# Token-major attention sums by DMA transposition instead of TensorE products, part of their normalisation on GpSimd, and plain full products instead of column tiles

## The chip, the cores and the metric

The kernel runs on one core of one Trainium2 chip. The metric is the device time of one execution in microseconds (us). Each time is the median of several executions. A ratio is the mean time of one kernel's fast runs over the mean time of the other's fast runs of the same rounds, so it is not quite the ratio of the medians quoted beside it; a 95% interval follows it in brackets. "Faster" and "slower" are verdicts at 2%.

## The reference, cut to what matters

A transformer block of 2048 tokens, width 640, 32 heads of 20, in four segments of 512 tokens. Each segment has causal softmax attention within itself, mixed by a gate with a read-out of a running linear memory of the earlier segments. A projection, two residuals and an MLP of width 1728 follow.

```python
for s in range(4):
    p = softmax(qs @ ks.T * scale + mask)
    a_dot = p @ vs                                  # the "P.V" sums
    num = phi(qs) @ M;  den = phi(qs) @ z + 1e-06   # memory read-out
    o = g * (num / den) + (1.0 - g) * a_dot
    M = M + phi(ks).T @ vs;  z = z + phi(ks).sum()
h  = x + o @ wo
h2 = h + silu(layernorm(h) @ w1) @ w2
```

Inputs and weights are bf16. The softmax denominator is summed as one more column of V and divided out at the end.

## The kernel before

A list of some 400 named tasks fixes the order of all engines; each engine runs its own tasks strictly in that order. A letter in the list picks the engine (`/D` VectorE, `/A` ScalarE, `/G` GpSimd). Heads go in eight groups of four for each segment, so groups 8 to 31 belong to segments 1 to 3. In this document a "group" is one of these.

For a group, TensorE computes P.V in four column tiles, feature-major (features on partitions). ScalarE or VectorE evicts the sums (copies them out of PSUM, the memory of TensorE's results) to `oTs` in SBUF, the working memory, scaled by the gate. TensorE then turns them token-major with identity products, into one PSUM bank, while the memory read-out goes to a second bank. VectorE normalises both halves together, and GpSimd adds them:

```python
def e_tn(eng):                                   # "tn": PE
    for i in range(b0, b1):
        for q, (c, m) in enumerate(bl):          # memory read-out, bank 1
            fns.append(lambda e, ...: e.matmul(bank(pp, 1)[:, V4*i:V4*i+V4],
                lhsT=phiQ[:, c, 128*i:128*i+128], rhs=Mzb[:, m, :], ...))
    for i in range(b0, b1):                      # transposition, bank 0
        fns.append(lambda e, i=i: e.matmul(bank(pp)[:, V4*i:V4*i+V4],
            lhsT=oTs[:, ots.slot, 128*i:128*i+128], rhs=sel, ...))
...
def e_nm(eng):                                   # "nm": DVE, both halves
    T.add(DV, lambda e: e.tensor_tensor(out=r2, in0=v[:, :, :, DH], in1=epsg, op=ALU.add))
    T.add(DV, lambda e: e.reciprocal(out=r2, in_=r2))
    T.add(DV, lambda e: e.tensor_tensor(out=on, in0=v[..., 0:DH], in1=r2, op=ALU.mult))
def e_ad(eng):                                   # "ad": GpSimd
    T.add(PO, lambda e: e.tensor_tensor(out=o_dst, in0=on[0], in1=on[1], op=ALU.add))
```

GpSimd also applies the causal mask ("mk") to the exponentials `PTA`, `PTB`, `PTE`, and P.V waits for that mask.

A full 128x128 product is issued as four column tiles where the neighbouring TensorE tasks are tiled too:

```python
for i, t in enumerate(real):
    before = real[i - 1].mode if i else "r"
    behind = real[i + 1].mode if i + 1 < len(real) else "F"
    t.cm = t.mode == "c" or t.mode == "F" and (before + behind in ("cc", "cr", "rc"))
```

The softmax here doesn't subtract the row's maximum and nothing guards it: scores larger than these inputs give would overflow.

## Time and profile before

| | before |
|---|---|
| time, median of 3 runs | 305.85 us (305.24 to 308.31) |
| TensorE busy, of a span of 306.1 us (the profiled execution took 307.81) | 291.2 us; so it stands still for 14.9 us |
| VectorE, ScalarE, GpSimd busy | 226.1, 220.0, 143.5 us |
| granted TensorE clock | 1.00, but 0.91 from 20 to 60 us |

The prediction below shows the page, the stretches and the timelines. One view that it doesn't show is the waits of TensorE alone. Its columns are: the instruction that waited and what released it, then the us waited in total, the times, and the longest. The first two lines are:

```profile
PE ps_all L896 <- ACT PTE L907: 1.4, 4, 0.7
PE ps_all L530 <- issue: 1.3, 8, 0.2
```

No wait of TensorE in this kernel is worth over 1.5 us, and GpSimd is not among the first ten releasers.

### The profile page before, as it was taken

What the parts mean: (1) busy time and instruction counts of PE and PEld (TensorE: products, weight loads), DVE (VectorE), ACT (ScalarE), POOL (GpSimd) and SP (SyncE); (2) the same over time, 40 slices, a digit from 0 to 9 for tenths busy, and PEclk for the clock granted to TensorE, in tenths of its full rate; (3) what the DMA queues carried; (4) which work ended last, traced back from release to release, by engine and by line L of the source; (5) the groups of instructions that cost most, each with busy time, mean ns of one, the idle gap of its engine ahead of it and who ended that gap; (6) DMA issues with size and microseconds to landing.
All of it is one profiled execution on the core that took longest, in us unless ns stands there. A gap on an engine that the chain in (4) does not pass through costs nothing.

```text
span 306.1 us, 8438 instructions
## 1 busy us (share of the span) xinstructions
PE 291.2 (95%) x3520; PEld 171.2 (56%) x3544; DVE 226.1 (74%) x496; ACT 220.0 (72%) x233; POOL 143.5 (47%) x280
## 2 busy tenths in 40 slices
PE   8989789999999999999999999999999999999996
PEld 6445435546665455576653544546665556764574
DVE  6677767898599896879998978886764696634623
ACT  4689959899989898995899798879768831003500
POOL 6145746375558766281736638464675530300000
PEclk9999879999999999999999999999999999999999
DMA  7949675660455111242433410144052014131002
GB/s 217 329 122 212 141 209 173 120 76 5 76 92 76 22 41 42 39 92 57 88 71 108 78 24 2 21 89 75 5 59 32 2 30 101 46 83 66 0 24 86
DMA packets 48581, 24.72 MB, mean 81 GB/s; under 512 B 38880, under 2 KB 47456, under 8 KB 48544
## 3 DMA queue, kind: packets, MB, share of 16 engines
q1 hardware_dynamic: 48544, 24.19, 35.5%
q8 instruction: 28, 0.46, 0.6%
q14 instruction: 9, 0.07, 0.1%
HBM read 10.41 MB, written 2.62 MB: 43 GB/s over the span
## 4 chain that ended last, share of the span: by engine, by line
PE 66%; DVE 14%; ACT 9%; DMA 6%; issue 3%; SPq 2%; ACTq 0%
PE ps_all L530 44%; PE ps_all L532 8%; PE ps_all L896 6%; PE ps_all L942 4%; DMA beta_bc<-in_A_beta_dram 4%; ACT PTA L907 3%; ACT PTB L907 2%; ACT PTE L907 2%; DMA x_tok<-in_A_x_dram 2%; DVE stt L720 2%; DVE on L1008 2%; PE ps_all L971 2%; DVE phiQ L849 1%; PE ps_all L975 1%; DVE sT L1176 1%
## 5 line engine op out<-in xcount | busy, mean ns | idle before, releaser
L907 ACT ACTIVATE PTA<-ps_all 128x2048 bf16<-128x2048 f32 x32 | 60.1, 1878 | 4.5 <-PE ps_all L896 4.2
L907 ACT ACTIVATE PTB<-ps_all 128x2048 bf16<-128x2048 f32 (+1 forms) x32 | 56.6, 1770 | 8.6 <-PE ps_all L896 8.5
L1170 ACT ACTIVATE th<-ps_all 128x512 f32<-128x512 f32 (+2 forms) x70 | 33.3, 501 | 39.0 <-PE ps_all L530 29.6
L919 POOL TENSOR_SCALAR_AFFINE_SELECT PTB<-PTB 128x512 bf16<-128x512 bf16 x64 | 41.3, 646 | 39.4 <-ACT PTB L907 37.1
L530 PE MATMUL ps_all<-w_sb,sT 128*128 128x320 bf16 x400 | 57.7, 299 | 0.5 <-DVE x_tok L1133 0.5
L530 PE MATMUL ps_all<-hT,w_sb 128*128 128x512 bf16 (+1 forms) x281 | 53.7, 338 | 1.1 <-DVE sT L1176 0.4
L1176 DVE SCALAR_TENSOR_TENSOR sT<-th,ps_all 128x512 bf16<-128x512 f32 (+2 forms) x70 | 37.8, 558 | 21.0 <-ACT th L1170 19.9
L530 PEld LDWEIGHTS ps_all<-w_sb,sT 128*128 128x128 bf16 x400 | 37.9, 98 | 17.6 <-issue 1.7
L530 PEld LDWEIGHTS ps_all<-hT,w_sb 128*128 128x128 bf16 x290 | 27.2, 98 | 22.9 <-issue 1.6
L907 ACT ACTIVATE PTE<-ps_all 128x2048 bf16<-128x2048 f32 (+1 forms) x20 | 34.1, 1707 | 6.4 <-PE ps_all L896 6.0
L919 POOL TENSOR_SCALAR_AFFINE_SELECT PTE<-PTE 128x512 bf16<-128x512 bf16 x40 | 26.2, 654 | 17.7 <-ACT PTE L907 16.3
L720 DVE BATCH_NORM_STATS2 stt<-x_tok 128x6 f32<-128x320 bf16 x64 | 27.8, 475 | 3.8 <-DMA x_tok<-in_A_x_dram 3.7
L1016 POOL TENSOR_TENSOR otok<-on 128x320 bf16<-128x320 bf16 x24 | 19.5, 812 | 18.7 <-DVE on L1008 18.7
L833 DVE CAST QK<-ps_all 128x512 bf16<-128x512 f32 x29 | 19.7, 686 | 8.8 <-PE ps_all L530 7.4
L1209 DVE SCALAR_TENSOR_TENSOR x_tok<-ps_all,x_tok 128x640 bf16<-128x640 f32 (+1 forms) x17 | 13.1, 780 | 12.8 <-PE ps_all L530 12.7
L896 PE MATMUL ps_all<-QK 20*128 20x256 bf16 (+3 forms) x360 | 20.5, 286 | 2.0 <-ACT PTE L907 1.3
L729 POOL TENSOR_TENSOR rst<-mvt,eps_c 128x1 f32<-128x1 f32 x32 | 6.5, 202 | 33.8 <-DVE mvt L723 33.8
L530 PE MATMUL ps_all<-xT,wqr 128*128 128x512 bf16 (+1 forms) x87 | 20.9, 368 | 0.9 <-issue 0.6
L919 POOL TENSOR_SCALAR_AFFINE_SELECT PTA<-PTA 128x512 bf16<-128x512 bf16 x24 | 15.7, 657 | 11.2 <-ACT PTA L907 10.9
L1008 DVE TENSOR_TENSOR on<-ps_all,rd 128x640 bf16<-128x640 f32 x24 | 19.8, 824 | 0.8
L530 PE MATMUL ps_all<-xT,wkr 128*128 128x512 bf16 x73 | 19.1, 394 | 1.1 <-issue 0.5
L731 POOL TENSOR_TENSOR rst<-rst,eps_c 128x1 f32<-128x1 f32 x32 | 18.6, 580 | 2.5
(92 smaller groups left out, 462.8 us busy)
## 6 DMA issues: line engine op xcount, KB each, us to landing
out_dram<-x_tok SPq DMA_DIRECT2D x15, 160.0 KB, 1.9
w_sb<-in_B_w_dram SPq DMA_DIRECT2D x5, 432.0 KB, 5.4
x_tok<-in_A_x_dram SPq DMA_DIRECT2D x3, 640.0 KB, 10.8
w_sb<-in_B_w_dram SPq DMA_DIRECT2D x3, 480.0 KB, 5.1
QKV<-QK SPq DMA_DIRECT2D x16, 72.0 KB
sT<-in_A_wq_dram SPq DMA_DIRECT2D x1, 800.0 KB, 5.9
sT<-in_A_wk_dram SPq DMA_DIRECT2D x1, 800.0 KB, 7.7
wv_sb<-in_A_wv_dram SPq DMA_DIRECT2D x1, 800.0 KB, 9.2
```

What stands on the lines that cost most here:

```text
L530: return [lambda e: e.matmul(out(), lhsT=lhsT(), rhs=rhs(), start=start, stop=stop)]
L532: return [lambda e, r=r: e.matmul(out()[m * r:m * r + m, :], lhsT=lhsT()[:, m * r:m * r + m], rhs=rhs(), start=start, stop=stop, tile_posi ...
L720: T.add(DV, lambda e, hh=hh: e.bn_stats(out=stt[:, s, 6 * hh:6 * hh + 6], in_=xb[:, 320 * hh:320 * hh + 320]), reads=R((xa, xsub)), writes ...
L731: T.add(PO, lambda e: e.tensor_tensor(out=rst[:, s, :], in0=rst[:, s, :], in1=eps_c[:, 1:2], op=ALU.pow), reads=R((st, ["r"]), (C, ["half" ...
L833: (lambda e: e.tensor_copy(out=o, in_=i_))
L896: fns.append(lambda e, j=j, o=o, r=r, q0=q0, q1=q1, qa=qa, ka=ka: e.matmul(ps_all[:, o:o + q1 - q0], lhsT=ka[32 * r:32 * r + DH, 128 * j:1 ...
L907: T.add(AC, lambda e: e.activation(out=pt[:, pta.slot, q0:q0 + 4, 0:width], in_=sc3[:, b0:b0 + 4, 0:width], func=ACT.Exp, scale=SCALE), re ...
L919: fns.append(lambda e, v=v: e.affine_select(out=v, in_=v, pattern=[[0, 4], [1, 128]], compare_op=ALU.is_ge, fill=0.0, base=0, channel_mult ...
L1008: T.add(DV, lambda e: e.tensor_tensor(out=on[:, ona.slot, :, :].rearrange("p b (x e) -> p b x e", e=DH), in0=v[:, :, :, 0:DH], in1=r2.unsq ...
L1016: T.add(PO, lambda e: e.tensor_tensor(out=o_dst, in0=on[:, ona.slot, 0, :].rearrange("p (i x) -> p i x", i=4), in1=on[:, ona.slot, 1, :].r ...
L1170: T.add(AC, lambda e: e.activation(out=th[:, tha.slot, lo:hi], in_=bank(ps)[:, lo:hi], func=ACT.Tanh, scale=0.5), reads=R((ps, [0])), writ ...
L1176: T.add(DV, lambda e: e.scalar_tensor_tensor(out=sT[:, f, lo:hi], in0=th[:, tha.slot, lo:hi], scalar=1.0, in1=bank(ps)[:, lo:hi], op0=ALU. ...
```

## The change

The intent is to take the 96 identity products off the bound engine. In segments 1 to 3 the P.V sums go token-major by a DMA transposition from SBUF to SBUF (`td`). The memory read-out then needs one PSUM bank instead of two. Its normalisation stays on VectorE (`nm`), and a new task (`nl`) normalises the local half from SBUF: ten of the 24 on VectorE, with its reciprocal, and 14 on GpSimd, where the reciprocal is written as a power with exponent -1. Full products are always plain, and the task order is made anew. The new order also shifts seven evictions of P.V sums from ScalarE to VectorE, as the prediction counts.

```diff
-            t.cm = t.mode == "c" or t.mode == "F" and (before + behind in ("cc", "cr", "rc"))
+            t.cm = t.mode == "c"
...
-            pp = G.alloc("ps", 2 if s else 1)
+            pp = G.alloc("ps", 1)
+            if s:
+                ota = G.alloc("oto")
+                dma(f"td{tag}", [(ots, [0])], [(ota, [0])],
+                    lambda e: e.dma_start_transpose(out=oto[:, ota.slot, :, :], in_=oTs[:, ots.slot, :]), ...)
...   (e_tn: the identity products only for segment 0; e_nm: the memory half alone)
+                def e_nl(eng):
+                    v = oto[:, ota.slot, :, :].rearrange("p i (r e) -> p (i r) e", e=32)
+                    if eng == DV:
+                        T.add(DV, lambda e: e.reciprocal(out=r2(0), in_=v[:, :, DH]), ...)
+                    else:
+                        T.add(PO, lambda e: e.tensor_tensor(out=r2(0), in0=v[:, :, DH],
+                                  in1=eps_c[:, 2:3].to_broadcast([128, 16]), op=ALU.pow), ...)
+                    T.add(eng, lambda e: e.tensor_tensor(out=o2(0), in0=v[:, :, 0:DH],
+                              in1=r2(0).unsqueeze(2).to_broadcast([128, 16, DH]), op=ALU.mult), ...)
+                G.task(f"nl{tag}", {DV: 0.25 + dve_c(320), PO: 1.5}, e_nl, ...)
...   (ORDER: the whole list of tasks is replaced)
```

## The prediction

> **What bounds the kernel now.** I read the page first (busy shares, slices), then the stretches of 20 us, the chain that ended last, PE's own timeline, and at last the tiles that the change touches.
>
> The page and the view by stretches (columns: stretch, length, busy us and instructions of each engine, granted clock, DMA share, GB/s):
>
> ```profile
> PE 291.2 (95%) x3520; PEld 171.2 (56%) x3544; DVE 226.1 (74%) x496; ACT 220.0 (72%) x233; POOL 143.5 (47%) x280
> ...
> PE 66%; DVE 14%; ACT 9%; DMA 6%; issue 3%; SPq 2%; ACTq 0%
> ```
>
> ```profile
> 20.00:40.00 20.00, 16.97 (x247) 9.46 (x247) 15.58 (x41) 17.36 (x16) 13.25 (x28) 0.91 0.70 149
> 40.00:60.00 20.00, 18.74 (x268) 10.10 (x270) 14.86 (x39) 17.27 (x17) 9.33 (x21) 0.91 0.68 180
> ...
> 180.00:200.00 20.00, 19.73 (x226) 10.07 (x227) 16.62 (x29) 18.11 (x17) 13.88 (x21) 1.00 0.07 13
> ...
> 260.00:280.00 20.00, 19.95 (x130) 12.55 (x130) 9.09 (x20) 1.33 (x3) 3.18 (x8) 1.00 0.22 50
> ```
>
> PE is busy for nearly all of every stretch after 60 us, and it is 66% of the chain; ACT is at about 90% while there is attention (to some 245 us), then nearly idle. So TensorE sets the end, with ACT close behind. But matmuls overlap, so I don't take busy time for work; I take the step from one start to the next. PE's timeline (start, length, engine, line, operation, count):
>
> ```profile
> 206.01 0.40 PE L896 MATMUL ps_all<-QK 20*128 20x512 bf16 x4
> 206.33 1.54 PE L532 MATMUL ps_all<-wo_sb,oT 128*32 128x320 bf16 x40
> 207.70 0.72 PE L1154 MATMUL ps_all<-hT,w_sb 128*32 128x256 bf16 x20
> 208.25 0.39 PE L942 MATMUL ps_all<-PTA,Vx 128*32 128x512 bf16 x4
> ```
>
> ```profile
> 192.92 0.63 PE L971 MATMUL ps_all<-Mzb,phiQ 128*128 128x84 bf16 x12
> 193.39 0.32 PE L975 MATMUL ps_all<-ident,oTs 128*128 128x84 bf16 x4
> 193.54 1.52 PE L530 MATMUL ps_all<-wv_sb,xT 128*128 128x320 bf16 x10
> 195.00 0.40 PE L896 MATMUL ps_all<-QK 20*128 20x512 bf16 x4
> 195.32 0.85 PE L530 MATMUL ps_all<-wv_sb,xT 128*128 128x320 bf16 x5
> ```
>
> What to see: L971 and L975 step at 0.47/12 = 39 and 0.15/4 = 38 ns. Ten full products of 320 columns take 1.46 us when scores follow them, and 40 column tiles (the same ten products) take 207.70 - 206.33 = 1.37 us when another column-tiled task follows. Four row-tiled score matmuls of 512 columns take 0.32 us, where their columns at 2.4 GHz ask 0.216. So a task followed by one of another tiling (row tiles, column tiles, full array) costs about 0.1 us more; one followed by its own kind costs nothing.
>
> **What the Trainium skill says.** "TensorE: Matmul & The Clock Gate", Back-to-back issue gap: an isolated step is N/2.4 + 2.5 ns. That is 37.5 ns for 84 columns and 135.8 for 320; the trace agrees (38 to 39; 1.37/10). The same section's sustained figure of about 131 ns for 512 columns is not what I see: five take 1.09 us (190.86 less 189.77 in PE's timeline), 218 each. "TensorEngine Tiling (Array Packing)", Restrictions: column tiling disables Fast Weight Load. The trace shows no loss from that here (1.37 us for either form), so undoing the column tiles of full products gains nothing by itself. "VectorE: DVE Perf Modes", The three transpose paths: 390 ns through TensorE against 1309 ns by DMA for 128x128. In this trace the DMA form of 128x512 lands 2.9 us after issue, and a TensorE product of that kind occupies PE for 38 ns: the change trades throughput of the bound engine for latency elsewhere. "GPSIMD Reference", Key points: GpSimd shares its SBUF interfaces with VectorE. The before trace has steady GpSimd times (787 to 963 ns for the add of `on`), so no strong contention now.
>
> **The change part by part.**
>
> *TensorE, removed.* For each of 24 head groups of segments 1 to 3, four identity products of 84 columns (L975): 96 x 38 ns = 3.65 us. The other 32 of L975 belong to segment 0 and stay.
>
> *TensorE, added.* 28 tasks that ran as column tiles beside the P.V sums become plain (14 of the MLP, 6 projections, 4 v, 4 wo). Their own time is the same, but they no longer bridge. Counting in the two task orders where neighbouring PE tasks differ in tiling: 186 before, 211 after. 25 x 0.1 = +2.5 us. Filler matmuls: 51 before, 50 after.
>
> *TensorE, the sum.* Counts of the program times N/2.4 + 2.5 ns: projections 43.2, v 21.7, wo 21.7, MLP up 58.5, MLP down 60.8, scores 17.4, P.V 17.4, identity 4.8, memory read 5.4, memory update 5.2, first transposes 1.1, fillers 5.6, together 262.9 us; plus 186 x 0.1 = 281.5. After: 259.2 + 21.1 = 280.3. **Net -1.2 us.** The run lasts 306, so some 22 us are start, cold fillers (30 took 5.3 us, not 3.3), the clock of 0.91 for 40 us (3.6 us) and about 15 us of waits. About half of the waits lie before 60 us, in segment 0, where the change takes no work away; the rest are spread over 190 us.
>
> *VectorE.* The tile views of `on` and `rd`, and GpSimd's power (name, count, ns min/median/max):
>
> ```profile
> L1002 DVE TENSOR_TENSOR rd<-ps_all,epsg x24: 174/183/192, 89.9 to 247.3; 128x32 f32<-128x32 f32 x24
> L1007 DVE RECIPROCAL rd<-rd x24: 352/353/353, 90.1 to 247.5; 128x32 f32<-128x32 f32 x24
> L1008 DVE TENSOR_TENSOR on<-ps_all,rd x24: 823/824/825, 90.5 to 247.9; 128x640 bf16<-128x640 f32 x24
> ```
>
> ```profile
> L731 POOL TENSOR_TENSOR rst<-rst,eps_c x32: 549/551/744, 4.5 to 267.7; 128x1 f32<-128x1 f32 x32
> ```
>
> Today a group costs 183 + 353 + 824 = 1.36 us. The memory half alone: about 170 + 250 (between 353 for 32 and 198 for 8 reciprocals) + 490 (a 320-column PSUM operation, L1209's short form, takes 492) = 0.91. That is -0.45 x 24 = -10.8 us. Ten groups do the local half on VectorE too: (250 + about 450) x 10 = +7. Seven more evictions of the P.V sums move from ScalarE to VectorE: about +4 there and -4 on ScalarE. VectorE is therefore about unchanged in total, ScalarE 2% lighter.
>
> *GpSimd.* 14 groups do the local half there: a power of 16 columns and a product of 320. The add of 320 takes 791 ns, the power of one column 551, against 192 for the add of one column. I take 1.5 us a group: +21 us, 143 to about 164. Its masks gate P.V, so 1.5 us at the wrong moment can hold PE.
>
> *DMA.* 24 more transposes on the one SP queue, where a transpose occupies the issuer for 1.2 us: +29 us of in-order issue, and 59 becomes 83 transposes. P.V's result reaches `otok` after eviction 0.7, transposition 2.9, local half 1.2 to 1.5 and add 0.8, where today it is eviction, 0.15 of PE, 1.36 and 0.8: about 3 us later. With the two buffers of `oTs` freed only when the DMA has landed, the next pair of groups (some 12 us later) should find them free.
>
> *PSUM.* The read-out holds one bank, not two, beside a score tile of four.
>
> *Start.* The first score exponential now waits 1.05 us on ScalarE behind the landing of beta; the new order puts that work after it. But 40 instead of 30 cold fillers stand before the first transposes. I call this even.
>
> *End.* After the last P.V task the new order has 14.7 us of PE work before the first wo of segment 3 (before: 13.2). The path beside it: eviction 0.7, transposition 2.9 with another 1.2 behind it, then on GpSimd earlier local halves and adds (5.4) and the last two groups (4.6), transposition of `otok` 2.6: some 13 us. It fits, with under 2 us to spare. After the last wo there are 8.4 us of PE work (13 before) over a norm chain of some 8 us. I allow +1 us here.
>
> Sum: -1.2 on PE, about +1 at the end, unchanged in the middle but for a little relief of PSUM: **305.0 us**, next to 305.85.
>
> **The rivals.** (a) *The waits shrink*: one bank more, ScalarE lighter by 4 us, VectorE's PSUM pass halved, so that half of the 7 to 9 us of waits between 60 and 245 go as well. For it: the chain has VectorE runs at 86 to 94, 108 to 115 and 157 to 173 us. Against: VectorE's total is not lower. About 300 us. (b) *GpSimd or the SP queue takes over*: the power of 16 columns may cost far more than that of one (359 ns above an add for each column would be 6 us), or transpositions queue behind the loads and one another and the masks and `otok` come late. For it: power is the dearest small operation in the trace, and the queue's waits are long. Against: GpSimd has half of the span free. 310 to 325 us. (c) *The mode changes cost more than 0.1 us*: at 0.2 us the balance is +1.4; 307 us.
>
> **Range and chances.** The arithmetic moves PE by -0.4%; what decides is how another order of 400 tasks meets real waits, some 1 to 2% either way, with a longer tail upward from (b). So 300.5 to 311.5; faster by over 2% (below 299.7) 0.1, slower by over 2% (above 312) 0.15.
>
> **What would show it.** 32 matmuls of L975's kind left, at 38 ns; PE busy some 288 us or more; an even count of about 25 more mode changes at 0.1 us each; VectorE near 226, ScalarE near 216, GpSimd near 164 us; new transpositions landing in 2.9 us, and the local half's power well under 1 us. The prediction is wrong if the power takes several us and the masks wait for it, if transpositions land in over 5 us, if PE stands still before the first wo of segment 3, or if the waits before 60 us change by more than 2 us.

## The result, and the profile after

The changed kernel took 331.08 us in the median; the kernel before, in the same rounds, took 305.69. The ratio of fast runs is 1.0791 [1.0689, 1.0892], **slower**, and outside the predicted range.

One of the four executions took 1328.11 us, and the first profile happened to be of it. In it TensorE was busy for 1322 us at a shown clock of 1.00, five products of 512 columns took 6.57 us (1.31 us each instead of 0.218), and the other engines' busy times were the usual ones. It did not recur in the four executions of the repeat run. I have no explanation for it and draw nothing from it. The other three took 329.16 to 332.32 us. Everything below is read from the repeat run's profile (experiment 1), at 329.90 us, with a span of 327.9.

The page of the changed kernel: busy time, then the chain that ended last, by engine and by line.

```profile
PE 298.9 (91%) x2868; PEld 165.6 (50%) x2868; DVE 223.2 (68%) x522; ACT 216.6 (66%) x227; POOL 193.5 (59%) x309
...
PE 42%; POOL 30%; ACT 9%; DVE 8%; DMA 7%; issue 2%; SPq 2%; ACTq 0%; POOLq 0%; DVEq 0%
PE ps_all L532 34%; POOL rd L1029 12%; POOL PTB L922 5%; PE ps_all L899 4%; POOL otok L1039 4%; DMA x_tok<-in_A_x_dram 4%; ACT PTB L910 3%; POOL on L1032 3%; PE ps_all L945 2%; ACT PTE L910 2%; POOL PTA L922 2%; ACT PTA L910 2%; POOL PTE L922 2%; DVE sT L1199 2%; DMA oto<-oTs 1%
```

Before, the chain was 66% TensorE and had no GpSimd in it. Now GpSimd is 30% of it, and one line of its code, L1029, is 12% of the span by itself. That line is the power. GpSimd is busy for 59% of the span, so its average still says nothing. The new transpositions (`oto<-oTs`) are 1% of the chain.

The tiles of the new local half (count, ns min/median/max) and its transposition:

```profile
L970 SPq DMA_TRANSPOSE oto<-oTs x24: 1188/1198/1792, 86.7 to 263.7; - x24
...
L1029 POOL TENSOR_TENSOR rd<-oto,eps_c x14: 2897/2907/3159, 96.9 to 269.6; 128x16 f32<-128x16 bf16 x14
L1032 POOL TENSOR_TENSOR on<-oto,rd x14: 726/727/728, 99.9 to 272.6; 128x320 bf16<-128x320 bf16 x14
```

The power of 16 columns takes 2.907 us, four times the product of 320 columns beside it. Fourteen local halves make 14 x (2.907 + 0.727) = 50.9 us, and GpSimd's busy time rose by 193.5 - 143.5 = 50.0.

The stretches of 20 us (length, busy us and instructions of TensorE, weight loads, VectorE, ScalarE, GpSimd, then granted clock, DMA share, GB/s):

```profile
40.00:60.00 20.00, 19.39 (x222) 9.77 (x219) 14.41 (x39) 15.62 (x15) 12.12 (x26) 0.86 0.42 90
...
100.00:120.00 20.00, 17.64 (x193) 9.42 (x192) 13.88 (x31) 16.62 (x18) 19.34 (x25) 1.00 0.23 46
...
180.00:200.00 20.00, 17.89 (x167) 8.69 (x166) 13.12 (x31) 14.54 (x14) 19.41 (x21) 0.91 0.29 43
...
260.00:280.00 20.00, 12.69 (x79) 7.17 (x77) 6.94 (x15) 2.93 (x5) 13.82 (x11) 0.86 0.27 60
```

The average of 59% hides stretches in which GpSimd is full: 19.34 and 19.41 us of 20. There TensorE is down to 17.6 and 17.9 us, where the kernel before had 18.86 and 19.73. From 260 to 280 TensorE works for only 12.69 us.

TensorE's waits after:

```profile
PE ps_all L945 <- POOL PTE L922: 6.0, 3, 2.8
PE ps_all L532 <- DMA oT<-otok: 4.7, 1, 4.7
PE ps_all L532 <- DVE on L1017: 3.8, 3, 1.8
```

None of these three was there before. The first is P.V waiting for a mask, the second the first `wo` product of segment 3 waiting for the last groups. How the power makes the first wait is seen in GpSimd's own timeline (start, length), and in the line of TensorE that it holds:

```profile
186.00 3.16 POOL L1029 TENSOR_TENSOR rd<-oto,eps_c 128x16 f32<-128x16 bf16 x1
189.24 0.73 POOL L1032 TENSOR_TENSOR on<-oto,rd 128x320 bf16<-128x320 bf16 x1
189.92 1.22 POOL L922 TENSOR_SCALAR_AFFINE_SELECT PTA<-PTA 128x512 bf16<-128x512 bf16 x2
191.09 1.34 POOL L922 TENSOR_SCALAR_AFFINE_SELECT PTE<-PTE 128x512 bf16<-128x512 bf16 x2
```

```profile
192.58 0.62 PE L945 MATMUL ps_all<-PTA,Vx 128*32 128x512 bf16 x4 [2.03 <-POOL PTE L922]
```

The masks stand behind 3.9 us of somebody else's local half. TensorE runs out of other work at 190.5 and stands for 2.03 us. The wait view names the mask as the releaser; the cause, the power, stands three lines further up on the same engine.

At the end the same happens to the groups themselves. From 255.54 to 274.22 us GpSimd works without a pause on local halves and adds, four of them with a power. Its last three instructions, and the product that waits:

```profile
269.65 2.90 POOL L1029 TENSOR_TENSOR rd<-oto,eps_c 128x16 f32<-128x16 bf16 x1
272.63 0.73 POOL L1032 TENSOR_TENSOR on<-oto,rd 128x320 bf16<-128x320 bf16 x1
273.43 0.79 POOL L1039 TENSOR_TENSOR otok<-on 128x320 bf16<-128x320 bf16 x1
```

```profile
276.91 2.85 PE L532 MATMUL ps_all<-wo_sb,oT 128*128 128x320 bf16 x10 [4.69 <-DMA oT<-otok]
```

After the last add comes a DMA transposition of some 2.6 us, and only then the first `wo` product of segment 3, at 276.91. In the kernel before that product starts at 254.51.

A stop costs more than its own length. The same columns in stretches of 2 us around the wait at 190.5 to 192.6:

```profile
190.00:192.00 2.00, 0.55 (x14) 0.20 (x11) 1.74 (x6) 0.74 (x2) 1.93 (x4) 1.00 0.00 0
192.00:194.00 2.00, 1.42 (x17) 0.66 (x18) 0.11 (x1) 0.05 (x1) 1.93 (x4) 0.62 0.00 0
194.00:196.00 2.00, 2.00 (x9) 1.18 (x8) 0.64 (x1) 1.82 (x1) 2.00 (x2) 0.52 0.09 19
```

After the stop the clock is at half for some 3.4 of the next 4 us: (1 - 0.62) x 2 + (1 - 0.52) x 2 = 1.7 us lost on top of 2.03 us of standing. The Trainium skill's "TensorE: Matmul & The Clock Gate", What's actually happening, describes this: a gate halves the clock after an idle window of about 3.4 us and gives it back after about as long a busy one. The trace agrees with the half and with the 3.4 us of recovery (3.4 at half would cost 1.7), but a stop of 2.03 us was enough here. Nor does every longer stop have this cost: after stops of 2.60 us (experiment 7) and 2.21 us (experiment 11, before 99.08 us) the clock stayed at 1.00. So the length of a stop alone doesn't decide it.

### The profile page after: what moved, and what is told of

It reads as the page before. It is cut to its first block, busy times and chain, and to the rows that moved or that the text cites. A ratio compares the mean times of both kernels' runs of the same rounds, so it can differ in the third digit from the quotient of the medians.

```text
span 1326.1 us, 7196 instructions
## 1 busy us (share of the span) xinstructions
PE 1322.1 (100%) x2868; PEld 438.7 (33%) x2868; DVE 222.1 (17%) x522; ACT 223.1 (17%) x227; POOL 191.6 (14%) x309
## 4 chain that ended last, share of the span: by engine, by line
PE 100%; DVE 0%; issue 0%
PE ps_all L532 79%; PE ps_all L899 7%; PE ps_all L945 7%; PE ps_all L1087 2%; PE ps_all L980 2%; PE ps_all L1177 1%; PE ps_all L984 1%; PE ps_all L749 0%; DVE x_tok L1232 0%; DVE zpad L594 0%
## 5 line engine op out<-in xcount | busy, mean ns | idle before, releaser
L532 PE MATMUL ps_all<-hT,w_sb 128*128 128x512 bf16 (+1 forms) x325 | 283.0, 1175 | 0.0
L532 PE MATMUL ps_all<-w_sb,sT 128*128 128x320 bf16 x448 | 268.0, 890 | 0.0
L532 PEld LDWEIGHTS ps_all<-w_sb,sT 128*128 128x128 bf16 x448 | 104.8, 236 | 156.8 <-issue 154.4
L532 PEld LDWEIGHTS ps_all<-hT,w_sb 128*128 128x128 bf16 x325 | 82.9, 260 | 172.2 <-issue 165.2
L532 PE MATMUL ps_all<-xT,wqr 128*128 128x512 bf16 (+1 forms) x105 | 129.8, 1552 | 0.0
L532 PE MATMUL ps_all<-xT,wkr 128*128 128x512 bf16 x100 | 128.8, 1593 | 0.0
L532 PE MATMUL ps_all<-wv_sb,xT 128*128 128x320 bf16 x160 | 122.9, 1096 | 0.0
L532 PE MATMUL ps_all<-wo_sb,oT 128*128 128x320 bf16 x160 | 109.1, 986 | 0.0
L899 PE MATMUL ps_all<-QK 20*128 20x256 bf16 (+3 forms) x360 | 65.0, 860 | 0.0
L945 PE MATMUL ps_all<-PTB,Vx 128*32 128x128 bf16 (+2 forms) x256 | 49.2, 909 | 0.0
```

The lines of the kernel that those rows point to most:

```text
L532: return [lambda e: e.matmul(out(), lhsT=lhsT(), rhs=rhs(), start=start, stop=stop)]
L899: fns.append(lambda e, j=j, o=o, r=r, q0=q0, q1=q1, qa=qa, ka=ka: e.matmul(ps_all[:, o:o + q1 - q0], lhsT=ka[32 * r:32 * r + DH, 128 * j:1 ...
L945: fns.append(lambda e, j=j, r=r, h=h, pa=pa, pt=pt, co=co, q0=q0, ji=ji: e.matmul(bank(po)[32 * r:32 * r + 32, q0:hi], lhsT=Vx[:, vx.slot, ...
```

## The experiments

T is the theory that the power's length, and where it stands on GpSimd, makes the loss. Its rivals are that the changes of tiling cost it, or that the transpositions and the rest of the new order do.

**1. The changed kernel again.** No edit.

> The changed kernel as it is, for a profile in the fast state: its only profile so far fell on an execution of 1328 us in which TensorE took 661 ns for a 256-column product from the first filler on. Theory A (GpSimd's power of 16 columns, measured at 2.9 us in that profile, holds the masks back): about 330 us, GpSimd at least 190 us busy, and long waits of the P.V products on GpSimd's masks. Rival B (the transpositions come late): the same time, but transpositions landing in 4 us or more and the local halves waiting for them. Rival C (tiling changes cost more than I took): the same time, PE busy throughout and no waits on masks. If the 1328 us belong to the program and not to one execution, one of the runs shows them again.

Measured: 329.79 us (328.26 to 330.18) against 305.44; ratio 1.0778 [1.0731, 1.0825]. All four executions agree, so the loss is real and the execution of 1328 us is not part of it.

**2. The reciprocal on VectorE, the product stays on GpSimd.**

```diff
-  T.add(PO, lambda e: e.tensor_tensor(out=r2(0), in0=v[:, :, DH], in1=eps_c[:, 2:3]..., op=ALU.pow), ...)
+  T.add(DV, lambda e: e.reciprocal(out=r2(0), in_=v[:, :, DH]), ...)
```

> The changed kernel with the reciprocal of the 14 local halves on VectorE (0.24 us each) in place of the power on GpSimd (2.9 us each); the product stays on GpSimd. Theory A: GpSimd loses 40.7 us, the time falls by most of the loss, to 304 to 312 us. Rival B (transpositions, queue order): 325 to 330 us. Rival C (tiling changes): 325 to 330 us.

Measured: 318.04 us, ratio 1.0421 [1.0362, 1.0481], correct. VectorE's reciprocal of 16 takes 0.24 us. This is outside the 304 to 312 us that T expected: not quite half of the loss is gone (from 7.8% to 4.2%), which by itself would leave the rest to a rival.

**3. The whole local half on VectorE.** In the list of tasks `nlX/G` becomes `nlX/D` for the 14 groups.

> The changed kernel with all 14 local halves wholly on VectorE: GpSimd loses 51 us, VectorE gains 14 x 0.74 = 10 us. Theory A: 304 to 313 us, a little better or worse than with the product left on GpSimd. Rivals B and C: 325 to 335 us.

Measured: 314.99 us, ratio 1.0314 [1.0262, 1.0366]. This too is just above what T expected. Here much of the rest has a plain cause. TensorE's first `wo` product of segment 3, and VectorE's line that it stood behind:

```profile
263.66 2.85 PE L532 MATMUL ps_all<-wo_sb,oT 128*128 128x320 bf16 x10 [6.31 <-DMA oT<-otok]
```

```profile
257.39 0.82 DVE L1232 SCALAR_TENSOR_TENSOR x_tok<-ps_all,x_tok 128x640 bf16<-128x640 f32 x1 [2.56 <-PE ps_all L532]
```

The list puts the local halves of the last two groups after an output sum (`o9`), which waits for an MLP product. On GpSimd that place costs nothing, because GpSimd has no part in `o9`. On VectorE the local halves stand behind it. This is an artifact of my edit, in experiment 2 as well, where the reciprocals have that place, and experiments 6 and 7 mend it.

**4. The kernel before with plain full products.** Nothing else of the change.

```diff
-            t.cm = t.mode == "c" or t.mode == "F" and (before + behind in ("cc", "cr", "rc"))
+            t.cm = t.mode == "c"
```

> The kernel before with its 28 column-tiled full products made plain and nothing else: 217 changes of tiling in PE's order in place of 186. At the 0.1 us that I read off, +3.1 us: 309 us. Theory A says 308 to 310. Rival C (a change costs much more, 0.5 us or so, and with it most of the loss of the changed kernel, which has 25 more changes): 320 us or more.

Measured: 306.32 us, ratio 1.0028 [0.9981, 1.0075], the same. This edit makes 31 more changes of tiling in the old order (186 to 217), more than the 25 of the change, and costs 0.0028 x 305.4 = 0.9 us, with an interval that holds zero. I had expected 308 to 310, so this is a miss, on the side that speaks against the rival of the tiling changes: about 0.03 us for each, and at most 0.0075 x 305.4 / 31 = 0.07 by the interval, where I had taken 0.1. Twenty-five of them can't make a loss of 25 us.

**5. A product in place of the power.** Everything else is as in the change. Its output is wrong, which doesn't matter for the time.

```diff
-  ... in1=eps_c[:, 2:3].to_broadcast([128, 16]), op=ALU.pow)
+  ... in1=eps_c[:, 2:3].to_broadcast([128, 16]), op=ALU.mult)
```

> The changed kernel with the 14 powers of 16 columns on GpSimd turned into products of the same operands: same engine, same place in every queue, same waits; the result is wrong on purpose. If the power itself takes the 2.9 us, and not the reading of 16 columns at a step of 64 bytes, one product takes 0.2 to 0.4 us. Theory A (the power, through GpSimd's order and through the clock that TensorE loses when it waits): 304 to 309 us. If something else in the change costs 9 us (the 9.5 us that stayed when the local halves went to VectorE): 313 to 316 us.

Measured: 304.07 us (302.14 to 304.87) against 305.78; ratio 0.993 [0.9867, 0.9992]. The page and the tile:

```profile
PE 288.4 (95%) x2842; PEld 163.5 (54%) x2868; DVE 225.4 (75%) x522; ACT 215.9 (71%) x227; POOL 157.5 (52%) x309
```

```profile
L1029 POOL TENSOR_TENSOR rd<-oto,eps_c x14: 215/222/391, 94.8 to 247.4; 128x16 f32<-128x16 bf16 x14
```

The same instruction, with the same operands in the same place, takes 0.222 us as a product. So neither its reading of every 32nd element nor the broadcast is the cost; the operation is. Without it the whole change takes 0.7% less than before, and the loss of 7.8% is gone. This is the experiment that decides for T: transpositions, tiling and order are all still in it.

The two spans also give the account of the loss. Experiment 1 spans 327.9 us and this one 302.5, a difference of 25.4. TensorE stands still for 327.9 - 298.9 = 29.0 us there and 302.5 - 288.4 = 14.1 here: 14.9 us of waits. Its mean clock is 0.969 there and 1.00 here: 0.031 x 327.9 = 10.2 us. Together 25.1. But 1.2 us are in both sums: from 274.4 to 276.9 us the clock is at half while TensorE stands still anyway. And not all of the clock is the power's: by the stretches, 3.4 us of it lie between 20 and 60 us ((1 - 0.97) x 20 and (1 - 0.86) x 20), before the first power at 96.9 us, in a place where the kernel before loses 3.6 in its profile. That leaves some 15 us of waits and, with 10.2 - 3.4 - 1.2, some 6 us of slow clock. The other three executions of experiment 1 had a mean clock of 0.974 to 0.979.

**6. The local half on VectorE, the last two groups before `o9`.** As experiment 3, and:

```diff
- ... td30:1 out7 th2_6_0:1 h1_2_8_0:7 s2_6_0 s2_9_0 ... h2_9_3 o9 nl31/G ad31 nl30/G ad30 ot14:0
+ ... td30:1 nl31/D ad31 out7 th2_6_0:1 h1_2_8_0:7 s2_6_0 nl30/D ad30 s2_9_0 ... h2_9_3 o9 ot14:0
```

> All local halves on VectorE as in the third experiment, and the last two (groups 31 and 30) with their adds taken out from behind the output add o9 in VectorE's order and put before it. In the third experiment TensorE stood still for 6.3 us before the first wo of segment 3 and then ran at a mean clock of 0.83 for 20 us (3.4 us): if that was made by my edit (VectorE's order has o9, which waits for the MLP product, ahead of the two halves; GpSimd's order had not), both go and the time is 304 to 307 us. If the tail is too short whatever the order (transposition, half, add, transposition), 311 to 315 us.

Measured: 309.18 us, ratio 1.0096 [1.0039, 1.0153]: the interval lies above one. So 5.8 us of experiment 3 was my order; the 304 to 307 us expected were missed by two.

**7. The reciprocal on VectorE, the last two groups before `o9`.** As experiment 2, with the same move.

> The second experiment (reciprocal on VectorE, product on GpSimd) with the same two last halves put before o9. Made by my edit: 304 to 308 us. Tail too short: 312 to 318 us.

Measured: 309.49 us, ratio 1.0131 [1.0065, 1.0198], just above the expected range. So 8.5 us of experiment 2 was my order. These two are the correct versions nearest to the kernel before, but some 5 us above experiment 5. In the profile of experiment 7 (span 305.9 us, against 302.5 in experiment 5's, both at a clock of 1.00) most of it arises in one place: from 180 to 200 us TensorE is busy for 15.95 us, where it was 18.99. GpSimd there, and TensorE behind it:

```profile
180.08 0.73 POOL L1030 TENSOR_TENSOR on<-oto,rd 128x320 bf16<-128x320 bf16 x1 [4.00 <-DVE rd L1028]
```

```profile
183.42 0.40 PE L944 MATMUL ps_all<-PTA,Vx 128*32 128x512 bf16 x4 [2.60 <-POOL PTE L921]
```

The product on GpSimd now waits 4.00 us for VectorE's reciprocal, and the masks wait behind the product.

**8. No power in the last stretch.** The powers of groups 26, 27, 28, 30 and 31 become reciprocals on VectorE, with the move of experiment 6; nine powers stay.

```diff
-                    if eng == DV:
+                    if eng == DV or k >= 26:
```

> The changed kernel with nine of its 14 powers left; the five of the last groups (26, 27, 28, 30, 31) become reciprocals on VectorE, the last two put before o9. If the loss were all in the tail: 305 to 309 us. If it is in the masks of segments 1 to 3: about 320 us. Theory A expects both, in parts of 8 to 12 us each: 317 to 322 us.

Measured: 320.24 us, ratio 1.0469 [1.0414, 1.0524]. Against experiment 1 the five powers of the last stretch, with the move, are worth (1.0778 - 1.0469) x 305.6 = 9.4 us, and the nine in the middle the rest of the way down to experiment 7, some 10, or to experiment 5, some 16. So the loss isn't in one place: both groups of powers have a share. No run takes them out one by one.

**9. The product later, for two groups.** As experiment 7, but the GpSimd product of groups 13 and 19 stands right before the add, so that GpSimd doesn't wait at 180 us.

> The seventh experiment with one more edit: in groups 13 and 19 the reciprocal stays where it is on VectorE, and the product on GpSimd goes behind the masks, right before the add. In the seventh, GpSimd stood 4.0 us in front of group 19's product, waiting for VectorE's reciprocal, with three pairs of masks behind it, and TensorE stood 2.6 us for the masks. If in-order waits of this kind are what is left over the multiply version (304.1 us): 305.5 to 308 us, about 2.5 us under the seventh's 309.5. If it is the added 3.4 us of VectorE work: 309 us or more.

Measured, with five rounds: 310.73 us, ratio 1.0149 [1.0116, 1.0183]. This is a miss: it is no better than experiment 7. The wait changed its place:

```profile
192.06 1.25 PE L531 MATMUL ps_all<-xT,wqr 128*128 128x512 bf16 x5 [3.38 <-DVE on L1016]
```

VectorE itself stood there for 3.9 us before its reciprocal, for the landing of the transposition. I did not settle how the remaining 5 us divide. No correct version that I ran beats the kernel before.

**10. The power cut in two, of 4 and of 12 columns.**

> The changed kernel with each power of 16 columns cut into one of 4 and one of 12. This measures how a power's time goes with its columns: from 0.55 us for one column and 2.9 us for 16, a straight line gives 0.157 us a column over a start of 0.39 us, so 1.02 us for 4 and 2.27 us for 12. If instead the reading of columns at a step of 64 bytes or the bf16 input had a large fixed part, 4 would take well over 1.3 us. The time should be 335 to 340 us, 14 x 0.4 us more than the changed kernel.

Measured: 334.83 us, one execution of unknown state. The groups by form (count, then busy us and mean ns, then idle before):

```profile
L1030 POOL TENSOR_TENSOR rd<-oto,eps_c 128x12 f32<-128x12 bf16 x14 | 32.2, 2300 | 1.1
L1030 POOL TENSOR_TENSOR rd<-oto,eps_c 128x4 f32<-128x4 bf16 x14 | 14.8, 1059 | 0.0
```

I had expected 1.02 and 2.27 us from a straight line. Eight columns more cost 2.300 - 1.059 = 1.24 us, 0.155 us a column, over a fixed part of 1.059 - 4 x 0.155 = 0.44 us. The one-column power of the kernel before (0.551 us) and the 16 columns here (2.907) lie on nearly the same line. Cutting it doesn't shorten it: the two parts take 3.36 us together.

**11. The kernel before, with the powers added.** A power of 16 columns from `rd` to a scratch tile ahead of the add, in the same 14 groups; its exponent is the -0.5 that lies ready, and its input f32 instead of bf16. The result is right and nothing uses the scratch.

```diff
+  if k in (8, 10, 11, 13, 17, 18, 19, 21, 25, 26, 27, 28, 30, 31):
+      T.add(PO, lambda e: e.tensor_tensor(out=pscr[:, :], in0=rd[:, rda.slot, 0:16],
+                in1=eps_c[:, 1:2].to_broadcast([128, 16]), op=ALU.pow), ...)
```

> The kernel before, with nothing of the change but one useless power of 16 columns on GpSimd ahead of the add in the same 14 groups (its result goes to a scratch tile, the output stays right). Theory A: GpSimd's order holds masks and adds back by 2.9 us at a time, with no transposition in it: 315 to 330 us. If the loss needs the new transposition chain around it, the kernel before takes the 41 us in GpSimd's idle time: 306 to 310 us.

Measured: 323.16 us (322.93 to 324.47) against 305.86; ratio 1.0565 [1.0525, 1.0606]. The power's tile (as long as in the change), and one stretch, in the kernel before and here:

```profile
L1018 POOL TENSOR_TENSOR pscr<-rd,eps_c x14: 2900/2913/3083, 93.4 to 261.8; 128x16 f32<-128x16 f32 x14
```

```profile
240.00:260.00 20.00, 19.88 (x178) 12.21 (x179) 14.84 (x28) 7.79 (x13) 4.63 (x7) 1.00 0.22 51
```

```profile
240.00:260.00 20.00, 19.16 (x215) 9.94 (x214) 12.98 (x26) 13.08 (x16) 19.05 (x17) 1.00 0.01 2
```

The old order, with no new transposition and no new tiling, loses 17.3 us to the powers alone, and GpSimd is full from 240 to 260 us (19.05 of 20, where it was 4.63). Fourteen powers add 14 x 2.91 = 40.8 us of GpSimd time, so 17.3 / 40.8 = 42% of it reaches the end. In the new order it is more, by experiments 1 and 5: 14 x (2.907 - 0.222) = 37.6 us of GpSimd time make 25.4 us of span, 68%.

## Why the prediction was wrong

**The step that failed is one term: "I take 1.5 us a group" for the local half on GpSimd.** It measured 2.907 + 0.727 = 3.63 us. The product was as the 320-column add suggested. The power was not under 1 us but 2.907. The kernel before shows the power of one column only (0.551 us), and from one point I chose for 16 columns a size of some 0.8 us, which treats nearly all of the 0.551 as a fixed cost. Experiment 10 shows it the other way round: most of the 2.907 goes by the column. The same point allowed up to 6 us, and the prediction says so as rival (b), names the engine, and lists both signs that came true: masks waiting for a power of several us, and TensorE standing before the first `wo` of segment 3. It gave a loss of over 2% a chance of 0.15, with the argument that "GpSimd has half of the span free". That was the second half of the mistake. Free time on average is no room at a given place on an engine that runs in order: GpSimd was full in two stretches, and the path at the end of the kernel, counted at 10.0 us of GpSimd work (5.4 and 4.6), was 18.7 us. Rival (b) itself stopped at 325 us; it names no term for the clock after a wait, some 6 us.

**TensorE's sum held.** 32 identity products are left, as said. With the power taken out (experiment 5) TensorE is busy for 288.4 us, at the foot of what the prediction names, and the kernel takes 0.993 of the time before, where the prediction's 305.0 over 305.85 is 0.997; the interval holds both. So the runs agree with a small gain, buried under the power. (The prediction's own terms, -1.2 and +1, give 305.65; the rest down to 305.0 is a relief of PSUM to which it gives no size.) That the gain comes from the 96 products is not shown: no run takes them out alone, the new order is in experiment 5 too, and the prediction itself allowed a new order 1 to 2% either way. Rival (a), shrinking waits, didn't come true: TensorE stands still for 14.1 us in experiment 5 and for 14.9 before.

**The tiling changes were oversized.** The term of +2.5 us (25 x 0.1) is more like 25 x 0.03 = 0.7 by experiment 4, which is within that run's error of nothing. The step of 0.1 us that the timeline shows at such places doesn't add up to the end in full.

**VectorE, ScalarE and DMA held.** VectorE: predicted about 226, measured 223.2. ScalarE: 216 and 216.6. The new transpositions: 2.9 us to landing, measured 2.5 in the median (2.4 to 4.3), and 1.2 us of issue each. TensorE's busy time before 60 us is 54.0 us against 53.1, so the start is even, as said.

**The end fell with the power.** "It fits, with under 2 us to spare" had the 1.5 us in it. (The terms listed there add up to 17.4 us; "some 13" holds where GpSimd's 5.4 us run beside the eviction and the two transpositions, as they did: GpSimd starts on them at 255.54 us, during the last P.V task.) The first `wo` product of segment 3 starts at 253.60 us with a product in place of the power, at 254.51 before, and at 276.91 in the changed kernel.

What stays open: why one execution took 1328 us, when a stop of 2 to 3 us halves the clock, and how the 5 us between experiments 5 and 7 could be won back in a correct kernel.

## What to carry to other kernels

When a small operation moves to another engine, its cost at the new width is the number to have first: a duration at one width doesn't tell the fixed part from the part for each column, and here one reading of 0.551 us gave under 1 us, another 6, and it was 2.9. Judge the room on an in-order engine by its busiest stretch and by what stands behind the new work there, not by its mean, and allow for what the clock may take after a wait of 2 us or more (here 1.7 us after 2.03, but nothing after 2.60 in another run). To find which part of a large change costs, keep the whole change and replace one operation by a cheap one of the same shape, even if the result is wrong; moving the operation to another engine brought new waits of its own and at first hid half of the answer.

## What the Trainium skill lacked or had wrong

- "GPSIMD Engine Reference", Elementwise — side-by-side cycle accounting, gives 4497 ns for an fp32 add of 2048 columns; no page has a figure for a power. Scaled to 320 columns that add is an estimate of 0.70 us; here a bf16 add took 0.79 and the product 0.727, so it is near. A power took 2.907 us for 16 columns: about 0.155 us a column over some 0.44 us, where a product of the same operands took 0.222.
- "TensorE: Matmul & The Clock Gate", What's actually happening, asks for an idle window of some 3.4 us before the clock halves. Here a stop of 2.03 us was followed by a clock of 0.62 and 0.52 over two stretches of 2 us, while stops of 2.21 and 2.60 us in other runs were not. The cost of about 1.7 us for one window at half clock agrees with the page.
- "VectorE: DVE Perf Modes", The three transpose paths, has the DMA transposition of 128x128 at 1309 ns. No page has the issue and the landing of one from SBUF to SBUF of 128x512 in a running kernel: 1.2 us of the queue and 2.5 us to landing.
- No page has the cost of a change of tiling between neighbouring TensorE tasks in a full kernel: 31 more of them cost 0.9 us, not told apart from zero.
